# Where SyncE issues the stores of a weight conversion that runs inside attention

## The chip, the core and the metric

One core of a Trainium2 chip. Lower is better: the metric is the device time of one execution in microseconds (us), the median of the runs of a kernel. Names used below: TensorE (PE in the profile, its weight loads PEld), VectorE (DVE), ScalarE (ACT), GpSimd (POOL), SyncE (SP; it computes nothing and issues transfers, and rows of its queue are marked SPq).

## What is computed

Attention with its heads mixed before and after the softmax, and behind it a two-layer network on the result, all in float32:

```python
scores = scale * np.matmul(q, k.transpose(0, 1, 3, 2))
scores = np.einsum('bhij,hg->bgij', scores, w_pre)
attn = np.exp(scores - np.max(scores, axis=-1, keepdims=True))
attn = attn / (np.sum(attn, axis=-1, keepdims=True) + 1e-09)
attn = np.einsum('bhij,hg->bgij', attn, w_post)
x = np.matmul(attn, v)          # (8, 12, 448, 64), then reordered to (3584, 768)
h = x @ w_in                    # (768, 2048)
out = (h - np.tanh(h)) @ w_out  # (2048, 768)
```

The weights `w_in` and `w_out` come as float64. The chip computes on float32, so each weight is first turned into two float32 parts whose sum it is.

## The kernel before

**Two stages.** Attention runs first, on queries in blocks of 120 or 88 rows, and the network behind it, seven products in place of eight for a pair of token blocks. The conversion of the weights has nothing to do with attention. It is threaded into attention's work so that VectorE, ScalarE and GpSimd do it beside what they do for attention.

**Places.** Attention is a loop of 180 places (`for p in range(NPL + 3)`, L1256). In place `p` TensorE mixes the heads of two groups of score rows (`premix`, L918, into PSUM), VectorE takes their maximum (L927), ScalarE the exponential (L929), VectorE and GpSimd make the weights of the second mixing out of the sums (`norm`: VectorE L938 and L939, then GpSimd `wr` L940), and TensorE does the second mixing for place `p - 1` (`mix`, L957). Score blocks (L874) and products with v (L999) fill the rest of TensorE's time. A call `in_order` (L134) fixes that each engine, SyncE too, works in the order in which the program was written.

**Transfers.** The score rows that `premix(p)` needs are gathered by SyncE into one of six buffers `t` (L907, two transfers a place), in place `p - 2`; a buffer becomes free when the `premix` three places before has read it. All other transfers go through lists: `queue` (q, k, v, and the results `xs`) and `slow` (everything of the conversion). `dma` appends an entry with the number of the present place, and `issue(6)`, called right behind the two gathers of a place, sends up to six entries that are older than the place's new number, first those of `queue`, then those of `slow` (L769 to L773, sent in `send`, L766). `conv.place()` stands ahead of the place's count in L1262, so what it appends is sent in the same place. `now()` (L1032) empties the lists; it is used before and behind the places.

**The conversion.** There are 48 quads (a quad is four blocks of 128 by 128 weights), 24 of `w_in` and then 24 of `w_out`. `Convert.place()` starts a quad about every 3.25 places, at least three places apart, and carries each one on by one step a place:

- place k: VectorE L81, L82 on the loaded tile `cr`
- place k+1: GpSimd L84, ScalarE L85
- place k+2: VectorE L90, L91, L94; L90 is the first write to the quad's tile `co`
- place k+3: GpSimd L96, L97
- place k+4: ScalarE L100, and GpSimd's sums (L116 to L119, or L128 to L130), the first write to the tile `ct`
- place k+5: GpSimd L103 and L105, then the entry of the store of `co` (L106)
- place k+6: GpSimd L108, then the entry of the store of `ct` (L109)

```python
    nc.gpsimd.tensor_sub(ol, m, raw(oh))                                    # L103
    ...
    dma(dst, raw(o).rearrange("p x t n -> p x (t n)"))                      # L106
    yield
    nc.gpsimd.tensor_sub(t[:, :, 1].bitcast(F32R), t[:, :, 1], t[:, :, 0])  # L108
    dma(sums_dst, t.rearrange("p s t n -> p s (t n)"))                      # L109
```

`co` and `ct` have two buffers each (`bufs=2`), `cr` has three. The first write to a buffer waits until the store that last read it has landed: L90 of a quad waits for the store of `co` of the quad two before it. Both stores and both loads of a quad (512 KB each store, 256 KB each load) are entries of the one list `slow`.

Of the kernel before, what the change touches and what calls it, by code (L numbers as in the profile page):

```python
# [21 lines left out]
def raw(ap):  # L22

    return ap.bitcast(F32)
# [10 lines left out]
class Convert:  # L35


    def __init__(self, nc, pool, dma, items, places):
        self.nc, self.pool, self.dma = nc, pool, dma
        self.todo, self.loads, self.active = list(items), [], []  # L40
        self.rate, self.due = len(self.todo) / places, 1.0

# [7 lines left out]
    def place(self):  # L50
        for x in list(self.active):
            next(x[0], None)
            x[1] += 1
            if x[1] == 7:
                self.active.remove(x)
        self.due = min(self.due + self.rate, 1.3)
        if self.due >= 1.0 and len(self.active) < 2 and not [x for x in self.active if x[1] < 4] and self.loads and self.loads[0][1]():
            r, _, to = self.loads.pop(0)
            self.active.append([narrow_quad(self.nc, self.pool, self.dma, r, *to), 1])
            next(self.active[-1][0])  # L60
            self.due -= 1.0
        if self.todo and len(self.loads) < 2 and len(self.loads) + len([x for x in self.active if x[1] < 5]) < 3:
            self.load()
# [5 lines left out]
            between()  # L69


def narrow_quad(nc, pool, dma, r, dst, sums, sums_dst):

    p = r.shape[0]
    hi, lo = r[:, :, :, 1], r[:, :, :, 0]
    u, w = hi, lo


    lim = 122879.9921875
    m = pool.tile([p, 4, 128], F32, name="cm", tag="cm", bufs=2)  # L80
    nc.vector.tensor_scalar(m, hi.bitcast(F32), lim, -lim, op0=ALU.min, op1=ALU.max)  # L81
    nc.vector.tensor_scalar(w, lo, 8, None, op0=ALU.logical_shift_right)  # L82
    yield
    nc.gpsimd.tensor_scalar(m, m, 2.0**-112, None, op0=ALU.mult)  # L84
    nc.scalar.mul(w.bitcast(F32), w, 2.0**-44)  # L85
    yield
    o = pool.tile([p, 4, 2, 128], F32R, name="co", tag="co", bufs=2)
    oh, ol = o[:, :, 0], o[:, :, 1]
    s = ol.bitcast(I32)
    nc.vector.tensor_scalar(s, hi, -(2**31), None, op0=ALU.bitwise_and)  # L90
    nc.vector.scalar_tensor_tensor(  # L91
        out=u, in0=m.bitcast(I32), scalar=3, in1=s, op0=ALU.logical_shift_left, op1=ALU.bitwise_or
    )
    nc.vector.tensor_scalar(s, u, -(2**23), None, op0=ALU.bitwise_and)  # L94
    yield
    nc.gpsimd.tensor_tensor(out=m, in0=w.bitcast(F32), in1=s.bitcast(F32), op=ALU.mult)  # L96
    nc.gpsimd.tensor_tensor(out=m, in0=m, in1=u.bitcast(F32), op=ALU.add)  # L97
    yield
    t = pool.tile([p, 4, 2, 128], F32, name="ct", tag="ct", bufs=2)
    nc.scalar.copy(oh, m)  # L100
    done = sums(nc, m, t[:, :, 1])
    yield
    nc.gpsimd.tensor_sub(ol, m, raw(oh))  # L103
    done()
    nc.gpsimd.tensor_copy(t[:, :, 0].bitcast(F32R), t[:, :, 1])  # L105
    dma(dst, raw(o).rearrange("p x t n -> p x (t n)"))  # L106
    yield
    nc.gpsimd.tensor_sub(t[:, :, 1].bitcast(F32R), t[:, :, 1], t[:, :, 0])  # L108
    dma(sums_dst, t.rearrange("p s t n -> p s (t n)"))  # L109


def sums_in(nc, m, t):
# [38 lines left out]
def kernel_body(  # L151
# [11 lines left out]
    nc = tc.nc  # L163
# [38 lines left out]
    quads = []  # L202
# [97 lines left out]
    class Gate:  # L300

        def __init__(self, h, own_mask=True):
            self.h, self.own_mask = h, own_mask
# [66 lines left out]
    class Results:  # L370
# [145 lines left out]
        def store(self, b, t, h, c):  # L516
            to = out[b * TB + t * TT : b * TB + (t + 1) * TT, h * N2 : (h + 1) * N2]
            eng = nc.gpsimd if self.n_gr < len(self.grs) else nc.sync
            eng.dma_start(to, c.rearrange("p c n -> p (c n)"))
# [216 lines left out]
    with ExitStack() as st:  # L736
# [4 lines left out]
        cv = early.enter_context(tc.tile_pool(name="cv", bufs=1, side="left"))  # L741
# [12 lines left out]
        kks, vts, krs, qrs, qbs, sts, ats = {}, {}, {}, {}, {}, {}, {}  # L754


        queue, slow, sent = [], [], {}

        def dma(dst, src, to=None):
            entry = [place[0], dst, src, None]  # L760
            (queue if to is None else to).append(entry)
            return lambda places=0: entry[3] is not None and entry[3] + places <= place[0]

        def send(x, engine):
            entry = x.pop(0)
            engine.dma_start(*entry[1:3])  # L766
            entry[3] = place[0]

        def issue(most):  # L769
            for x in (queue, slow):  # L770
                while x and most and x[0][0] < place[0]:
                    send(x, nc.sync)
                    most -= 1  # L773

        place = [0]

        def load_k(b, hq, t=None):
            if t is None:
                t = ld.tile([CP, NC, 4, D], F32, name="kr", tag="kr", bufs=2)

            sent[b, hq, "k"] = dma(t, k[b, 4 * hq : 4 * hq + 4].rearrange("h (p c) d -> p c h d", c=NC))
            krs[b, hq] = t

        def load_v(b, hq):
            t = kp.tile([CP, 4, NC, D], F32, name="vr", tag="vr", bufs=3)
            sent[b, hq, "v"] = dma(
                t.rearrange("p h c d -> p h (c d)"),
                v[b, 4 * hq : 4 * hq + 4].rearrange("h (p c) d -> p h (c d)", c=NC),
            )
            vts[b, hq] = t  # L790

        def load_q(i, t=None):
            b, m = blocks[i]
            if t is None:
                t = ld.tile([MT, H, D], F32, name="qr", tag="qr", bufs=1)
            sent[i, "q"] = dma(t[: sizes[m]], q[b, :, starts[m] : starts[m] + sizes[m], :].rearrange("h p d -> p h d"))
            qrs[i] = t
# [234 lines left out]
        def now(*engines):  # L1032
            place[0] += 1
            engines = engines or (nc.sync,)
            for x in (queue, slow):
                while x:
                    send(x, engines[len(x) % len(engines)])


        load_q(0)  # L1040
        now()
        for hq in range(3):
            load_k(0, hq, kp.tile([CP, NC, 4, D], F32, name="tmp_k", tag="x", bufs=1) if hq == 2 else None)
        now()
        load_q(1, kp.tile([MT, H, D], F32, name="tmp_q", tag="at", bufs=2))
        now()
        for hq in range(3):
            load_v(0, hq)
# [32 lines left out]
        for w in range(2):  # L1081
            for at in AT[w]:
                x = repeat[:, w, at : at + HP].rearrange("p (i h) -> p i h", i=GH)
# [7 lines left out]
        for w in range(2):  # L1091
            for a in range(2):
                if w == 0:
                    x = both[:, w, a].rearrange("p (i g) -> p i g", i=GH)
                    of, step = ps_w[:, w, :].unsqueeze(1).to_broadcast([P, GH, H]), [[H, GH], [0, H]]
                else:
                    x = both[:, w, a].rearrange("p (g i) -> p g i", i=GH)
# [41 lines left out]
        place[0] += 1  # L1139
        scores_of(1, 0)  # L1140
        NPL = NG // 2
        conv = Convert(nc, cv, partial(dma, to=slow), quads, NPL - 24)

# [19 lines left out]
        at_s, p, kind = {}, 0, None  # L1165
        window = {i: (lo, hi) for lo, hi, k, i, _ in sorted(halved, reverse=True) if k == "s"}
        while halved:
            ready = sorted((x for x in halved if x[0] <= p), key=lambda x: (x[1], x[3:]))
            if ready:
                x = ready[0]  # L1170
# [3 lines left out]
                if x[2] == kind and other and x[1] > p + 1:  # L1174
                    x = other[0]
                halved.remove(x)
                _, _, kind, i, n = x
# [23 lines left out]
        for i, (b, m) in enumerate(blocks):  # L1201
            p0 = first[i] // 2
            if i + 2 < len(blocks):
                p = at_s[i + 2, 0] - 1
# [7 lines left out]
        for b in range(1, B):  # L1212
            p, o, done = first[blocks.index((b - 1, 1))] // 2 - 4, 0, []
            for hq in range(3):
                if hq == 2:

                    p = max(p, done[0] + 1)
                at_place(p, load_k, b, hq)
                o = max(p + 4, o + 1)
                p += 1  # L1220
                if hq > KB - 4:

                    o = max(o, end_s[blocks.index((b - 1, 3)), hq - 1 - (KB - 4)] + 1)
# [32 lines left out]
        for p in range(NPL + 3):  # L1256
# [6 lines left out]
            for t in (2 * p + 4, 2 * p + 5):  # L1263
                if t < NG:
                    gather(t)
            issue(6)
            if p == NPL + 1:
                for f in start.pop(p):
# [56 lines left out]
    for s in range(NS):  # L1325
# [24 lines left out]
        n = HELD[s] + AHEAD[s]  # L1350
# [44 lines left out]
```

## Time and profile before

| | |
|---|---|
| median of 3 runs | 1708.94 us (1706.41 to 1719.01) |
| the profiled execution | 1703.0 us, its span 1701.3 us |
| granted TensorE clock, mean | 0.994 |
| TensorE busy | 1660.1 us, 98% of the span |
| VectorE, ScalarE, GpSimd busy | 1231.3, 1091.1, 585.5 us |
| places, first to last `premix` | 25.2 to 838.8 us |
| the conversion, first L81 to last store issued | 51.5 to 781.5 us |

The page gives the busy time of each engine, the waits give for each engine and line how long it stood still and what ended that, in total, with the number of times and the longest. The timeline lists instructions by start and duration in us; a row of SPq is the time in which SyncE issues a transfer, not that of the transfer. The chain of work that ended last also has pieces that begin with DMA: a transfer from its issue to its landing.

### The profile page before, as it was taken

How to read it: one execution, taken by the hardware profiler on the slowest of the kernel's cores; microseconds unless marked ns; L12 is line 12 of the kernel's file. 1: busy time of each engine (PE TensorE's matmuls, PEld its weight loads, DVE VectorE, ACT ScalarE, POOL GpSimd, SP SyncE). 2: the span in 40 equal slices, each digit the busy share in tenths (PEclk: the TensorE clock that was granted, in tenths of full speed). 3: DMA queues.
4: the chain of work that ended last, by engine and by line, in shares of the span. 5: the costliest groups of instructions: out<-in, count | busy, mean ns of one | idle time of the engine just before them, and what ended most of it. 6: DMA issues, size and time to landing. Idle time of an engine off the chain costs nothing.

```text
span 1701.3 us, 41215 instructions
## 1 busy us (share of the span) xinstructions
PE 1660.1 (98%) x16068; PEld 1379.8 (81%) x16068; DVE 1231.3 (72%) x2119; ACT 1091.1 (64%) x1920; POOL 585.5 (34%) x798
## 2 busy tenths in 40 slices
PE   8999999999999899999999999999999999999999
PEld 6777777777777677677788888888888888989999
DVE  5777777878777777675497899868778867778432
ACT  5777777777777677676586777556667456666331
POOL 1466667666666666662100111101001101011100
PEclk9999999999999999999999999999999999999999
DMA  8879889898987979856589899989999989988993
GB/s 183 218 228 257 255 246 276 247 270 259 256 253 231 269 234 257 254 182 208 190 269 340 273 331 318 346 295 335 318 334 362 368 272 327 326 311 327 404 413 132
DMA packets 322290, 475.09 MB, mean 279 GB/s; under 512 B 105264, under 2 KB 255280, under 8 KB 322096
## 3 DMA queue, kind: packets, MB, share of 16 engines
q1 hardware_dynamic: 305660, 414.34, 75.5%
q0 software_dynamic: 16128, 57.68, 8.7%
q8 instruction: 128, 2.10, 0.5%
q14 instruction: 66, 0.54, 0.1%
q10 hardware_dynamic: 308, 0.43, 0.1%
HBM read 274.73 MB, written 120.59 MB: 232 GB/s over the span
## 4 chain that ended last, share of the span: by engine, by line
PE 72%; DMA 7%; DVE 7%; ACT 4%; issue 4%; POOL 4%; SPq 1%; POOLq 0%; ACTq 0%; DVEq 0%
PE ps_o L957 11%; PE ps_h L291 8%; PE ps_h L292 7%; PE ps_h L294 7%; PE ps_m L999 6%; PE ps_p L918 6%; PE y L534 6%; PE y L532 6%; PE y L533 6%; PE ps_q L874 4%; DMA t<-s 2%; DMA gl<-gs 2%; ACT e L929 1%; DVE mx L927 1%; PE y L504 1%
## 5 line engine op out<-in xcount | busy, mean ns | idle before, releaser
L957 PEld LDWEIGHTS ps_o<-wr,e 60*112 60x112 f32 (+1 forms) x5760 | 303.3, 175 | 46.1 <-POOL wr L940 31.9
L957 PE MATMUL ps_o<-wr,e 60*112 60x60 f32 (+1 forms) x5760 | 314.5, 259 | 16.1 <-POOL wr L940 14.6
L929 ACT ACTIVATE e<-ps_p,mx 128x448 f32<-128x448 f32 x360 | 224.8, 631 | 117.2 <-DVE mx L927 82.8
L927 DVE TENSOR_REDUCE mx<-ps_p 128x1 f32<-128x448 f32 x360 | 206.5, 615 | 109.1 <-PE ps_p L918 108.5
L967 ACT COPY at<-ps_o 112x960 f32<-112x960 f32 x156 | 154.3, 989 | 103.4 <-PE ps_o L957 102.9
L918 PE MATMUL ps_p<-t,wpre 60*64 60x448 f32 (+1 forms) x1440 | 182.4, 570 | 6.7 <-DMA t<-s 6.6
L999 PEld LDWEIGHTS ps_m<-at,vr 112*64 112x64 f32 x3072 | 147.6, 137 | 23.0 <-issue 7.7
L999 PE MATMUL ps_m<-at,vr 112*64 112x120 f32 (+1 forms) x3072 | 161.4, 262 | 1.1 <-DMA vr<-in_v_dram 0.9
L532 PE MATMUL y<-w,gh 128*128 128x384 f32 x448 | 151.2, 338 | 2.1 <-DMA w<-wo 1.6
L940 POOL TENSOR_TENSOR wr<-wpost,zs 128x120 f32<-128x120 f32 x180 | 70.0, 389 | 237.6 <-DVE zs L939 199.0
L533 PE MATMUL y<-w,gh 128*128 128x384 f32 x448 | 150.5, 336 | 0.0
L534 PE MATMUL y<-w,gl 128*128 128x384 f32 x424 | 143.4, 338 | 3.0 <-DVE gl L450 3.0
L874 PEld LDWEIGHTS ps_q<-kk,qh 64*120 64x120 f32 (+1 forms) x768 | 59.1, 174 | 82.0 <-issue 45.1
L874 PE MATMUL ps_q<-kk,qh 64*120 64x448 f32 (+1 forms) x768 | 121.8, 394 | 0.9 <-ACT kk L825 0.4
L879 DVE COPY s<-ps_q 120x448 f32<-120x448 f32 (+1 forms) x192 | 112.2, 614 | 9.8 <-PE ps_q L874 8.0
L669 POOL DMA_DIRECT2D gs<-gb x24 | 17.2, 717 | 291.6 <-DVE gb L668 291.6
L307 ACT ACTIVATE u<-h 128x1024 f32<-128x1024 f32 x56 | 59.5, 1063 | 74.4 <-DVE h L716 70.5
L879 ACT COPY s<-ps_q 120x448 f32<-120x448 f32 (+1 forms) x192 | 94.9, 538 | 7.1 <-PE ps_q L874 6.7
L647 POOL DMA_DIRECT2D gs<-ga x24 | 17.2, 716 | 230.0 <-DVE ga L330 222.9
L532 PEld LDWEIGHTS y<-w,gh 128*128 128x128 f32 x448 | 84.2, 188 | 7.2 <-issue 3.5
L533 PEld LDWEIGHTS y<-w,gh 128*128 128x128 f32 x448 | 84.1, 188 | 3.4
L534 PEld LDWEIGHTS y<-w,gl 128*128 128x128 f32 x424 | 79.6, 188 | 4.6 <-DVE gl L450 4.6
(372 smaller groups left out, 3971.3 us busy)
## 6 DMA issues: line engine op xcount, KB each, us to landing
t<-s SPq DMA_DIRECT2D x342, 210.0 KB
wa<-ss SPq DMA_DIRECT2D x96, 384.0 KB
w<-wo SPq DMA_DIRECT2D x43, 768.0 KB
gl<-gs SPq DMA_DIRECT2D x62, 512.0 KB
wa<-wi SPq DMA_DIRECT2D x72, 384.0 KB
w<-ts SPq DMA_DIRECT2D x35, 768.0 KB
gs<-gs POOLq DMA_DIRECT2D x24, 768.0 KB, 9.2
cr<-in_moe_w_in_dram SPq DMA_DIRECT2D x48, 256.0 KB
```

The lines of the kernel that those rows point to most:

```text
L291: nc.tensor.matmul(ph, w[:, c, 0], xh, start=start and c == 0, stop=False, skip_group_check=True)
L532: nc.tensor.matmul(y, gh[:, tok], wh, start=first, stop=False, skip_group_check=True)
L533: nc.tensor.matmul(y, gh[:, tok], wl, start=False, stop=False, skip_group_check=True)
L534: nc.tensor.matmul(y, gl[:, tok], wh, start=False, stop=last, skip_group_check=True)
L874: nc.tensor.matmul(ps[:n, :S], qx[a, hp, :], kx[a, hp % 2], start=(x == 0), stop=(x == 2))
L879: eng(sts[i][:n, 2 * hp + j, :], ps[:n, :S])
L918: nc.tensor.matmul(pss[r][halves[j], :], wpre[k, :], ts[j][k, :], start=True, stop=True)
L927: nc.vector.tensor_reduce(out=mx, in_=ps, axis=AX.X, op=ALU.max, negate=True)
L929: nc.scalar.activation(e, ps, AF.Exp, bias=mx, scale=1.0, accum_out=zs[:, 0, r : r + 1])
L957: nc.tensor.matmul(ps[:CP, j, c * GP : (c + 1) * GP].rearrange("p (h i) -> p h i", i=GI)[:, :, r * GH : (r + 1) * GH], e[k, c * CP : (c + ...
L967: nc.scalar.copy(ats[i0][:, :, :, at : at + 2 * GI].rearrange("p c h (j i) -> p j (c h) i", j=2), ps[:CP, :, : NC * GP].rearrange("p j (x ...
L999: nc.tensor.matmul(pv[j * D : (j + 1) * D, r, :n], vt[:, j, c, :], ats[i][:, c, 2 * hp + j, :n], start=(c == 0), stop=(c == NC - 1),)
```

## The change

The stores of the conversion get a list of their own, `out_q`, and an entry in it carries the number of the next place. `issue` and `now` serve it between `queue` and `slow`. A store is therefore sent one place later than the step that made its data, and the loads of the conversion, alone now in `slow`, are sent behind a store that falls due in the same place. No operation of a computing engine is added, removed or moved.

```diff
-    def __init__(self, nc, pool, dma, items, places):
-        self.nc, self.pool, self.dma = nc, pool, dma
+    def __init__(self, nc, pool, dma, store, items, places):
+        self.nc, self.pool, self.dma, self.store = nc, pool, dma, store
...
-            self.active.append([narrow_quad(self.nc, self.pool, self.dma, r, *to), 1])
+            self.active.append([narrow_quad(self.nc, self.pool, self.store, r, *to), 1])
...
-def narrow_quad(nc, pool, dma, r, dst, sums, sums_dst):
+def narrow_quad(nc, pool, store, r, dst, sums, sums_dst):
...
-    dma(dst, raw(o).rearrange("p x t n -> p x (t n)"))
+    store(dst, raw(o).rearrange("p x t n -> p x (t n)"))
     yield
     nc.gpsimd.tensor_sub(t[:, :, 1].bitcast(F32R), t[:, :, 1], t[:, :, 0])
-    dma(sums_dst, t.rearrange("p s t n -> p s (t n)"))
+    store(sums_dst, t.rearrange("p s t n -> p s (t n)"))
...
-        queue, slow, sent = [], [], {}
-
-        def dma(dst, src, to=None):
-            entry = [place[0], dst, src, None]
+        queue, slow, out_q, sent = [], [], [], {}
+
+        def dma(dst, src, to=None, behind=0):
+            entry = [place[0] + behind, dst, src, None]
...
         def issue(most):
-            for x in (queue, slow):
+            for x in (queue, out_q, slow):
...
         def now(*engines):
...
-            for x in (queue, slow):
+            for x in (queue, out_q, slow):
...
-        conv = Convert(nc, cv, partial(dma, to=slow), quads, NPL - 24)
+        conv = Convert(nc, cv, partial(dma, to=slow), partial(dma, to=out_q, behind=1), quads, NPL - 24)
```

The orders of TensorE, VectorE, ScalarE and GpSimd are the same in both programs; only SyncE's differs. It has two places below, in each of which two gathers (`t<-s`) open a place. The first is the place at about 151 us of the trace, where v and the next k are also loaded. `wi` is where the parts of `w_in` go, `ss` their sums. Before:

```order
L907 DMA t<-s 120x1x448 x2
L766 DMA qr<-in_q_dram 88x12x64
L766 DMA vr<-in_v_dram 112x4x256
L766 DMA wi_66<-co 512x1x256
L907 DMA t<-s 120x1x448 x2
L766 DMA vr<-in_v_dram 112x4x256
L766 DMA ss_78<-ct 512x1x256
L907 DMA t<-s 120x1x448 x2
L766 DMA kr<-in_k_dram 112x16x64
L766 DMA cr<-in_moe_w_in_dram 128x2x256 x2
```

With the change, from the same two gathers on:

```order
L907 DMA t<-s 120x1x448 x2
L766 DMA qr<-in_q_dram 88x12x64
L766 DMA vr<-in_v_dram 112x4x256
L907 DMA t<-s 120x1x448 x2
L766 DMA vr<-in_v_dram 112x4x256
L766 DMA wi_66<-co 512x1x256
L907 DMA t<-s 120x1x448 x2
L766 DMA kr<-in_k_dram 112x16x64
L766 DMA ss_78<-ct 512x1x256
L766 DMA cr<-in_moe_w_in_dram 128x2x256 x2
```

The store of `co` stands behind one more pair of gathers and a load of v. The store of `ct` now falls into the place of the next quad's two loads, and ahead of them. The second is the stretch that follows, before:

```order
L766 DMA cr<-in_moe_w_in_dram 128x2x256 x2
L907 DMA t<-s 120x1x448 x2
L766 DMA wi_67<-co 512x1x256
L907 DMA t<-s 120x1x448 x2
L766 DMA ss_79<-ct 512x1x256
L907 DMA t<-s 120x1x448 x2
L766 DMA cr<-in_moe_w_in_dram 128x2x256 x2
```

and with the change:

```order
L766 DMA cr<-in_moe_w_in_dram 128x2x256 x2
L907 DMA t<-s 120x1x448 x4
L766 DMA wi_67<-co 512x1x256
L907 DMA t<-s 120x1x448 x2
L766 DMA ss_79<-ct 512x1x256
L766 DMA cr<-in_moe_w_in_dram 128x2x256 x2
```

Where quads follow each other at three places, each place had one kind of the conversion's transfers (loads, `co`, `ct`); now one place has none, one has `co`, and one has `ct` and both loads.

## The prediction, as it was put on record

> **What bounds the kernel now.** The page comes first: TensorE is busy for 98% of the span. The second row below is that of the stretch 41 to 776 us in the view of windows (length, then the busy time of TensorE, its weight loads, VectorE, ScalarE and GpSimd), which holds nearly all of the conversion: 715.6 of 735 us.
>
> ```profile
> PE 1660.1 (98%) x16068; PEld 1379.8 (81%) x16068; DVE 1231.3 (72%) x2119; ACT 1091.1 (64%) x1920; POOL 585.5 (34%) x798
> ```
>
> ```profile
> 41.00:776.00 735.00, 715.59 (x10448) 549.17 (x10450) 547.42 (x1379) 528.20 (x1209) 483.75 (x615) 0.99 0.83 247
> ```
>
> So 19.4 us of that stretch are TensorE's idle time, and a change that leaves its work alone can win no more there. What ended that idle time stands in the waits of TensorE from 40 to 840 us (total, times, longest):
>
> ```profile
> PE ps_o L957 <- POOL wr L940: 13.4, 16, 1.7
> PE ps_p L918 <- DMA t<-s: 5.0, 7, 1.0
> ```
>
> The first row is the second mixing waiting for its weights, which come from VectorE over GpSimd. The second is the first mixing waiting for a gather that landed late. SyncE can shorten only the second: 5.0 us. Next, the waits in SyncE's own queue in the same stretch:
>
> ```profile
> SPq L907 <- PE ps_q L874: 130.4, 69, 5.0
> SPq L907 <- PE ps_p L918: 26.2, 28, 2.2
> ...
> SPq L766 <- POOL co L103: 14.4, 9, 4.4
> SPq L766 <- POOL ct L108: 13.1, 11, 4.7
> ```
>
> SyncE does stand before its transfers of L766 until GpSimd is done, 27.5 us in the two rows of the stores' own last steps, and it is in order, so the gathers of the next place stand behind it. But a gather mostly waits longer for TensorE to free its buffer (the first two rows).
>
> **What the change removes: SyncE's wait for GpSimd.** The timeline around 534 us shows one such wait and what it costs, first SyncE's rows, then one of GpSimd and one of TensorE:
>
> ```profile
> 530.33 2.03 SPq L907 DMA_DIRECT2D t<-s  x2
> 534.33 0.58 SPq L766 DMA_DIRECT2D ts<-ct  x1
> 535.89 1.59 SPq L907 DMA_DIRECT2D t<-s  x2
> ```
>
> ```profile
> 533.03 1.28 POOL L108 TENSOR_TENSOR ct<-ct 128x512 fp32r<-128x512 f32 x1
> ```
>
> ```profile
> 534.84 0.98 PE L918 MATMUL ps_p<-t,wpre 60*64 60x448 f32 x8
> ```
>
> SyncE is free at 532.36 and issues the store at 534.33, when L108 has ended (533.03 + 1.28 = 534.31): 1.97 us of waiting. It is free again at 534.91. The next gather goes out at 535.89 only, since the `premix` that frees its buffer ends at 534.84 + 0.98 = 535.82. Without the store's wait it would go out at the same time. This follows from the way a place is built: the gathers of a place need the `premix` of the place before, and GpSimd's step, recorded ahead of that `premix`, is over by then. So I take 0 us for the removed wait; the bounds are 0 and the 5.0 us by which TensorE waits for gathers at all. The issuing itself is only moved, 96 stores of some 0.6 us.
>
> **What the change moves: the stores land one place later.** A place lasts (838.8 - 25.2) / 179 = 4.55 us, from the first and last `premix` of 180:
>
> ```profile
> L918 PEld LDWEIGHTS ps_p<-t,wpre x1440: 128/132/229, 25.2 to 838.8; 60*64 60x64 f32 x172, 48*64 48x64 f32 x8
> ```
>
> ```profile
> L90 DVE TENSOR_SCALAR co<-cr x48: 407/418/1023, 59.2 to 761.5; 128x512 int32<-128x512 int32 x48
> ```
>
> L90 of a quad overwrites the `co` buffer of the quad two before, and must wait until that buffer's store has landed. Read off the timeline, 46 such pairs run from 8.3 to 18.9 us between the store's issue and L90, 13.5 us in the middle, and ten of them have 8.3 to 11.0 us. No wait of VectorE for a store of `co` is among its waits before, so all 46 fit. Take away a place and the ten are left with 3.8 to 6.5 us. (`ct` is first written two steps later than `co` and stored one later: it has a place more in hand, and I take 0 for it.) Two of the tightest pairs, with what hangs on L90 in each:
>
> ```profile
> 150.74 1.91 SPq L766 DMA_DIRECT2D wi<-co  x1
> ...
> 155.24 0.57 SPq L766 DMA_DIRECT2D ss<-ct  x1
> ...
> 159.46 0.41 DVE L90 TENSOR_SCALAR co<-cr 128x512 int32<-128x512 int32 x1
> ...
> 161.60 0.39 POOL L940 TENSOR_TENSOR wr<-wpost,zs 128x120 f32<-128x120 f32 x1 [2.66 <-DVE zs L939]
> ...
> 163.59 1.69 PE L957 MATMUL ps_o<-wr,e 60*112 60x60 f32 x32
> ```
>
> ```profile
> 567.12 0.44 SPq L766 DMA_DIRECT2D wo<-co  x1
> ...
> 570.14 6.12 SPq L766 DMA_DIRECT2D ts<-ct  x1
> ...
> 575.44 0.42 DVE L90 TENSOR_SCALAR co<-cr 128x512 int32<-128x512 int32 x1
> ...
> 578.07 0.39 POOL L940 TENSOR_TENSOR wr<-wpost,zs 128x120 f32<-128x120 f32 x1
> ...
> 581.31 0.87 PEld L957 LDWEIGHTS ps_o<-wr,e 60*112 60x112 f32 x16 [0.16 <-issue]
> ```
>
> In both, the store of `co` goes with the change to about where the store of `ct` stands now: 155.24 and 570.14. VectorE is then 4.2 and 5.3 us from L90. Behind L90 in VectorE's order stand L938 and L939, for these GpSimd's `wr`, for that TensorE's mixing. The first pair has 163.59 - 161.99 = 1.6 us to spare between `wr` and the mixing, the second 581.31 - 578.46 = 2.85. What L90 waits beyond that, TensorE waits too.
>
> How long does a store take to land? The trace tells it only where a transfer is on the chain of work that ended last (start, us from issue to landing):
>
> ```profile
> 156.75 9.32 DMA t<-s
> 194.27 3.24 DMA wi<-co
> 565.65 6.48 DMA t<-s
> 581.96 3.99 DMA wo<-co
> ```
>
> Stores in a quiet stretch: 3.24 and 3.99 us. Gathers in just the two crowded stretches above: 9.32 and 6.48 us. They give the bounds. With the place's 4.55 us added and compared with the 46 distances:
>
> - 3.24 us for all: no pair is short, 0 us.
> - 6.48 us: the ten tight pairs are short by 10.6 us in all; less 1.6 us to spare each time, 2.8 us reach TensorE.
> - 9.32 us: 26 pairs are short by 53.5 us, and 23.4 us reach TensorE.
>
> The tight pairs lie in crowded stretches (v, k and q are loaded there, and one issue took 6.12 us), so the nearest row is the crowded gather of the same stretch, 6.48 us, and I take 2.8 us. [...]
>
> **What it bunches.** The order of SyncE shows one place in three with a store of `ct` and both loads of the next quad, where each place had one kind. The gathers behind them land later, those of the empty place earlier. The bounds are the 5.0 us of TensorE's present waits for gathers, lost once more or won. Bunching leans to the loss; I take a fifth, 1.0 us.
>
> **Sum.** 0 + 2.8 + 1.0 = 3.8 us. On the profiled execution, 1703.0 us (span 1701.3), that is 1706.8 us. The median of the runs shown, 1708.94, lies 5.9 us above this execution, so I predict 1708.94 + 3.8 = 1712.7, put as 1713 us. A measurement of this kernel can tell about 1% (17 us) from no change; I forecast none that it can tell.
>
> **The rivals.**
>
> - *A lost transfer wait:* the conversion's wait was what made gathers late, and TensorE's 5.0 us go away: 1704 us. For it: the 27.5 us of SyncE's waits for GpSimd. Against it: around 534 us the gather's buffer sets the time.
> - *Nothing:* late stores land in 3.2 us as in the quiet rows, and L90 never waits: 1709 us. [...] Against it: the issue of 6.12 us and the 9.32 us landing.
> - *The reuse of `co` becomes the wait, everywhere:* stores take 9.32 us, VectorE stops at 26 of 46 quads, 23.4 us reach TensorE, with the bunching's 5.0 us 1737 us: slower. The point from which it decides is a landing of about 8.7 us in all pairs: by the same count 16.8 us reach TensorE there, 1%. For it: the first crowded row. Against it: two thirds of the pairs have more than 12 us and lie in quiet stretches, where the rows say 3.2 to 4.0.
> - *The change does not do what it says*, since `issue` sends six entries at most and a store could be pushed on: excluded by SyncE's order, where each store is exactly one place on.
>
> **How the numbers follow.** The forecast (a few L90 waits, 1709 to 1722 us) 0.60; nothing 0.18; gathers won 0.13; the reuse decides 0.08; a gain of over 1% 0.01, as it would need nearly all of the 19.4 us of idle time. The first three lie within 1%, 0.91, and I move a little to each side for what two medians of few runs differ by: faster 0.02, same 0.90, slower 0.08. The range goes down to the rival that wins gathers with a little of the runs' spread (1703) and up to a landing of 8 us in all pairs (10.0 us) with a part of the bunching (1723).
>
> **What would show it.** Right: in the changed kernel's waits a row of VectorE `co` L90 waiting for a DMA of `co`, about five to ten times with some 10 us in all, mostly near 160, 270, 380, 575 and 690 us; SyncE's rows of L766 waiting for GpSimd L103 and L108 nearly gone; TensorE's wait of L957 for `wr` some 2 to 5 us up, its wait for gathers between 3 and 8 us; and the last `premix` 2 to 8 us later than 838.8 us. The step on the removed wait is wrong if the gather row falls below 2 us. The step on `co` is wrong if VectorE never waits for a store there. The forecast as a whole is wrong if the time leaves 1703 to 1723 us.

## The result, and the profile after

| | before | after |
|---|---|---|
| median (10 runs each, taken together) | 1707.12 us | 1720.91 us |
| lowest to highest | 1702.51 to 1719.01 | 1709.83 to 1728.38 |
| the profiled execution | 1703.0 us | 1727.89 us |
| its span, its granted clock | 1701.3 us, 0.994 | 1726.2 us, 0.983 |

The ratio of the two kernels is 1.0063, with an interval from 1.0034 to 1.0092: the change costs 10.8 us (5.8 to 15.7). The medians alone differ by 13.8 us, inside that interval. The profiled execution of after is one of its longer runs.

**What one run's two numbers tell.** Each run lists its span and its mean granted clock. The table below splits the span into span x clock, about the time that the run would have taken at the full clock, since TensorE sets the time for nearly all of it (busy for 98% of the span of before, 97% of that of after), and span x (1 - clock), the time that the lower clock took. In after the first part lies between 1695.8 and 1699.6 us in all ten runs, so most of their spread, 18.5 us, is the clock. Means, with the standard deviation of one run:

| | runs | at the full clock | lost to the clock |
|---|---|---|---|
| before (beside the experiments) | 73 | 1692.5 us (1.5) | 14.5 us (3.4) |
| after | 10 | 1697.3 us (1.4) | 22.2 us (6.4) |
| difference | | +4.8 us | +7.7 us |

Three more runs of before, 1 to 7% longer at a lower clock, are left out of the 73. The first difference has an error of some 0.5 us, the second of some 2 us (the deviations over the square root of the number of runs). So the change costs in two ways, and for the second, which looks like the larger one, the prediction had no term.

**Where the profile of after shows it.** The last `premix` of attention, from the view of TensorE's line L918:

```profile
L918 PEld LDWEIGHTS ps_p<-t,wpre x1440: 129/132/228, 25.8 to 863.2; 60*64 60x64 f32 x172, 48*64 48x64 f32 x8
```

It was at 838.8 us before: 24.4 us, all but half a microsecond of the difference of the two executions (1726.2 - 1701.3 = 24.9), arise in attention. TensorE's waits there, from 40 us to the last `premix`:

```profile
PE ps_o L957 <- POOL wr L940: 16.4, 19, 2.3
PE ps_p L918 <- DMA t<-s: 5.3, 4, 2.0
PE ps_m L999 <- DMA vr<-in_v_dram: 3.3, 3, 2.2
```

The mixing's wait for `wr` went from 13.4 to 16.4 us, the gathers' from 5.0 to 5.3, and the product with v waits 3.3 us for its load, 0.9 before:

```profile
PE ps_m L999 <- DMA vr<-in_v_dram: 0.9, 1, 0.9
```

Together that is 25.0 against 19.3 us, 5.7 us more of standing still, about what the full-clock time says. Each row is that of one execution, though. In the kernels below in which SyncE's order is that of before (e6, e8, e9 and e11), TensorE waits 2.1 to 4.6 us for v, so the 3.3 us alone do not show an effect of the change. VectorE's waits in the same stretch of after:

```profile
DVE x L1017 <- DMA xs<-x: 5.3, 3, 3.2
DVE co L90 <- DMA wi<-co: 4.5, 4, 2.9
DVE co L90 <- DMA wo<-co: 2.8, 2, 2.5
```

The last two rows did not exist before: L90 stands six times, 7.3 us in all, until a store of `co` has landed. (The first row, 1.0 us before and 1.3 to 6.4 us in the four kernels just named, is a result of attention waiting for its buffer.) One of the six can be followed to TensorE, first in SyncE's timeline, then in that of the others:

```profile
159.68 0.51 SPq L766 DMA_DIRECT2D vr<-in_v_dram  x1
160.30 0.56 SPq L766 DMA_DIRECT2D wi<-co  x1
...
163.07 0.83 SPq L766 DMA_DIRECT2D kr<-in_k_dram  x1
164.00 5.22 SPq L766 DMA_DIRECT2D ss<-ct  x1
```

```profile
168.30 0.43 DVE L90 TENSOR_SCALAR co<-cr 128x512 int32<-128x512 int32 x1 [2.92 <-DMA wi<-co]
...
170.15 0.17 DVE L939 RECIPROCAL zs<-zs 128x2 f32<-128x2 f32 x1
170.46 0.39 POOL L940 TENSOR_TENSOR wr<-wpost,zs 128x120 f32<-128x120 f32 x1 [8.13 <-DVE zs L939]
...
170.90 0.80 PE L957 MATMUL ps_o<-wr,e 60*112 60x60 f32 x12 [2.33 <-POOL wr L940]
```

The store goes out at 160.30 between loads of v and k and releases L90 at 168.30, 8.0 us later. L90 waited 2.92 us for it, and two steps further TensorE has waited 2.33 us for `wr`. What follows is in the view of windows (length, busy time of TensorE, its weight loads, VectorE, ScalarE and GpSimd, then the granted clock, the DMA share and GB/s):

```profile
169.70:173.10 3.40, 2.20 (x40) 1.86 (x40) 2.98 (x11) 2.17 (x7) 2.64 (x3) 1.00 1.00 293
173.20:176.50 3.30, 3.30 (x30) 2.47 (x24) 1.31 (x3) 2.62 (x7) 3.14 (x7) 0.50 0.74 255
```

Behind the gap the granted clock is 0.50 for a stretch. So the wait cost its 2.33 us, and about half of 3.4 us once more, if the stretch is put down to it. In the profiled execution of after, such stretches up to the end of attention make up 16 times 3.41 us, in that of before 5 times: 11 x 1.7 = 18.8 us of the 24.4. That is more than the 7.7 us of the means: this execution of before lost less to the clock than most (10.4 us in its whole span), and this one of after more (29.0 us).

### The profile page after: what moved, and what is told of

Its sections match the earlier page's. It is cut to its first block, busy times and chain, and to the rows that moved or that the text cites. A ratio compares the mean times of both kernels' runs of the same rounds, so it can differ in the third digit from the quotient of the medians.

```text
span 1726.2 us, 41222 instructions
## 1 busy us (share of the span) xinstructions
PE 1678.0 (97%) x16068; PEld 1392.2 (81%) x16068; DVE 1233.7 (71%) x2119; ACT 1091.9 (63%) x1920; POOL 585.0 (34%) x798
## 4 chain that ended last, share of the span: by engine, by line
PE 74%; DVE 7%; DMA 7%; ACT 4%; issue 4%; POOL 3%; SPq 1%; POOLq 0%; ACTq 0%; DVEq 0%
PE ps_o L957 11%; PE ps_h L291 7%; PE ps_h L292 7%; PE ps_h L294 7%; PE ps_m L999 7%; PE ps_p L918 6%; PE y L532 6%; PE y L534 6%; PE y L533 6%; PE ps_q L874 4%; DMA wi<-co 2%; DMA t<-s 2%; ACT e L929 1%; DVE mx L927 1%; DMA w<-wo 1%
## 5 line engine op out<-in xcount | busy, mean ns | idle before, releaser
L957 PEld LDWEIGHTS ps_o<-wr,e 60*112 60x112 f32 (+1 forms) x5760 | 308.2, 177 | 50.2 <-POOL wr L940 35.7
L957 PE MATMUL ps_o<-wr,e 60*112 60x60 f32 (+1 forms) x5760 | 319.5, 261 | 18.9 <-POOL wr L940 17.6
L918 PE MATMUL ps_p<-t,wpre 60*64 60x448 f32 (+1 forms) x1440 | 185.7, 581 | 7.2 <-DMA t<-s 6.9
L999 PEld LDWEIGHTS ps_m<-at,vr 112*64 112x64 f32 x3072 | 152.0, 140 | 27.5 <-issue 8.8
L999 PE MATMUL ps_m<-at,vr 112*64 112x120 f32 (+1 forms) x3072 | 166.4, 266 | 3.4 <-DMA vr<-in_v_dram 3.3
L879 DVE COPY s<-ps_q 120x448 f32<-120x448 f32 (+1 forms) x192 | 112.6, 615 | 10.8 <-PE ps_q L874 10.1
```

The source lines that it names most:

```text
L879: eng(sts[i][:n, 2 * hp + j, :], ps[:n, :S])
L918: nc.tensor.matmul(pss[r][halves[j], :], wpre[k, :], ts[j][k, :], start=True, stop=True)
L957: nc.tensor.matmul(ps[:CP, j, c * GP : (c + 1) * GP].rearrange("p (h i) -> p h i", i=GI)[:, :, r * GH : (r + 1) * GH], e[k, c * CP : (c + ...
L999: nc.tensor.matmul(pv[j * D : (j + 1) * D, r, :n], vt[:, j, c, :], ats[i][:, c, 2 * hp + j, :n], start=(c == 0), stop=(c == NC - 1),)
```

## The experiments

The experiments of each group ran beside runs of the kernel before on the same chip; a ratio is to these. In the three groups the mean full-clock time of before is 1692.2, 1692.8 and 1692.5 us. The table sums the experiments up, as differences from the means of before above; an error of some 0.4 to 1.4 us belongs to the full-clock column and of 1 to 4 us to the other.

| kernel | runs | median | ratio (95%) | at full clock | lost to the clock |
|---|---|---|---|---|---|
| after | 10 | 1720.91 | 1.0063 (1.0034 to 1.0092) | +4.8 | +7.7 |
| e1_co3 | 12 | 1713.86 | 1.0044 (1.0021 to 1.0068) | +2.8 | +3.5 |
| e3_co_late | 6 | 1723.13 | 1.0103 (1.0065 to 1.0141) | +7.7 | +8.5 |
| e4_ct_late | 12 | 1710.13 | 1.0018 (0.9998 to 1.0038) | +0.1 | +2.2 |
| e5_two_late | 5 | 1753.01 | 1.026 (1.0238 to 1.0283) | +15.6 | +27.9 |
| e6_before_co3 | 12 | 1712.55 | 1.0007 (0.9987 to 1.0027) | +0.5 | +2.5 |
| e7_co_late_co3 | 7 | 1725.31 | 1.0086 (1.0054 to 1.0117) | +6.9 | +10.2 |
| e8_stall | 12 | 1711.14 | 1.0011 (0.9991 to 1.0031) | +2.0 | +0.8 |
| e9_norm_first | 6 | 1738.97 | 1.0155 (1.0126 to 1.0184) | +22.4 | +6.4 |
| e10_spread | 12 | 1711.03 | 1.0015 (0.9992 to 1.0038) | +0.9 | +1.8 |
| e11_before_fill | 12 | 1703.25 | 0.9961 (0.994 to 0.9982) | +2.5 | -7.7 |
| e12_after_fill | 12 | 1713.80 | 1.0015 (0.999 to 1.0041) | +6.9 | -2.5 |

The list `out_q` by itself, without the later number, leaves SyncE's order as it was before; it was not run. What is tested is the later place.

### e1_co3: the change with a third buffer of co

```diff
-    o = pool.tile([p, 4, 2, 128], F32R, name="co", tag="co", bufs=2)
+    o = pool.tile([p, 4, 2, 128], F32R, name="co", tag="co", bufs=3)
```

> The changed kernel with three co buffers in place of two, so that L90 waits for the store of the quad three before. Reuse theory (the late store of co makes VectorE wait at L90, TensorE stands still behind it, and the clock is granted at half after it): no wait of L90 for a DMA of co, and 0 to 4 us over the kernel before, where the change has 10.8. Bunching theory (the store of ct together with both loads makes gathers and loads of v land late): unchanged by the buffer, 8 to 14 us over before.

Measured: 1713.86 us. There is no row of L90 waiting for a store any more, and TensorE's waits are:

```profile
PE ps_o L957 <- POOL wr L940: 12.9, 15, 1.6
PE ps_p L918 <- DMA t<-s: 4.7, 5, 1.3
PE ps_m L999 <- DMA vr<-in_v_dram: 2.4, 3, 1.3
```

The wait for `wr` is back at what it was before (13.4). Against after, 2.0 us of full-clock time are gone (error 0.7) and 4.2 us of lost clock (error 2.6). So the reuse of `co` is real, and its stops have about the size that the prediction gave them; but 2.8 us of full-clock time stay, so it is not all. By the ratio e1 lies 7.5 us over before, between the ranges of the two theories.

### e3_co_late and e4_ct_late: one of the two stores late

```diff
-    store(sums_dst, t.rearrange("p s t n -> p s (t n)"))
+    store(sums_dst, t.rearrange("p s t n -> p s (t n)"), behind=0)
```

is e3: only `co` is late, and falls into the place of `ct`. In e4 the same `behind=0` stands at the store of `co` (L106): only `ct` is late, and falls into the place of the loads.

> Only the store of co goes a place later, that of ct stays in time; both then fall into one place, and the loads have a place of their own. Reuse theory: as the change, L90 waits 5 to 10 times, 5 to 10 us in all, 6 to 14 us over before. Bunching of ct with the loads: not there, 0 to 4 us over before.

> Only the store of ct goes a place later, into the place of the next quad's loads; that of co stays in time. Reuse theory: no wait of L90 for a DMA of co, 0 to 3 us over before. Bunching theory: 6 to 14 us over before, with TensorE's waits for gathers and for v at 8 us or more (6 us before).

Measured: e3 1723.13 us, e4 1710.13 us. With `co` alone late the kernel loses more full-clock time than with the whole change (+7.7 against +4.8 us), and by its ratio, 17.6 us over before, it lies above the ranges of both theories. L90 waits twice there, 5.8 us in all, and not 5 to 10 times. What both stores of a quad, 1 MB, in one place cost is the subject of e7. With `ct` alone late, 33 places hold `ct` and both loads, exactly as many as in after, and the mean full-clock time is that of before (+0.1 us, error 0.8). So on the mean those places by themselves are not what costs. Yet e4's profile shows the waits that the bunching theory had named, for v and gathers 11.0 us (8 or more were expected), TensorE's and then VectorE's from 40 to 850 us:

```profile
PE ps_m L999 <- DMA vr<-in_v_dram: 5.6, 5, 2.3
PE ps_p L918 <- DMA t<-s: 5.4, 6, 1.4
```

```profile
DVE x L1017 <- DMA xs<-x: 5.6, 3, 3.3
```

The profiled execution has 1696.0 us of full-clock time, 3.5 more than the mean of before; the twelve runs of e4 go from 1689.0 to 1698.0 us. So in that execution the waits cost time, and the other runs of e4 need not have had them. A profile of one execution does not say what a kernel pays on the mean.

### e5_two_late: both stores two places late

```diff
-partial(dma, to=out_q, behind=1)
+partial(dma, to=out_q, behind=2)
```

> Both stores two places later in place of one. The 46 distances from the store of co to L90 lose another 4.5 us and are 2 to 10 us, against a landing of 5.7 us at the median. Reuse theory: L90 waits at half of the quads or more, 50 us or more of VectorE's time in all, and 25 to 60 us over before. Bunching theory: co in place of ct now falls in with the loads, the same amount, 8 to 14 us over before.

Measured: 44 us more. VectorE's and TensorE's waits from 40 to 890 us:

```profile
DVE co L90 <- DMA wi<-co: 16.7, 9, 4.8
DVE co L90 <- DMA wo<-co: 15.3, 5, 5.3
```

```profile
PE ps_o L957 <- POOL wr L940: 37.8, 22, 6.4
```

L90 waits 14 times, 32.0 us in all, fewer and less than expected (half of the quads, 50 us), and TensorE's wait for `wr` goes from 13.4 to 37.8 us. The time is in the range of the reuse theory. This is the rival in which the reuse decides, brought on by a second place. Of the 44 us, 27.9 are lost clock, where after, with 16.4 us of waits for `wr`, loses 7.7.

### e6_before_co3: the third buffer without the change

This is the kernel before with the one line of e1.

> The kernel before with three co buffers, SyncE's order as before: a control for the third buffer itself. If the 7 us that are left in the changed kernel with three buffers come from where the stores stand, this is 0 to 2 us from before, and the time at full clock (span times granted clock) within 1.5 us of the 1692 us of before. If the third buffer costs something by itself, 4 us or more over before.

Measured: ratio 1.0007, the interval on both sides of 1. The buffer by itself makes no difference that these runs can tell, so what e1 wins over after is the wait it takes away.

### e7_co_late_co3: co late, with the wait taken away

This is e3 with the one line of e1.

> Only the store of co late, with three co buffers: the kernel that alone cost 17.6 us, without the reuse. Reuse theory: no wait of L90 for co, time at full clock 3 us or less over before (8 us with two buffers), 2 to 7 us over before in all. Crowding theory (co and ct, 1 MB, in one place): time at full clock still 5 us or more over before, 10 us or more in all.

Measured: 1725.31 us, not better than e3. Its waits for transfers, TensorE's from 40 to 850 us, then VectorE's:

```profile
PE ps_m L999 <- DMA vr<-in_v_dram: 7.6, 6, 2.0
PE ps_p L918 <- DMA t<-s: 7.1, 6, 2.5
```

```profile
DVE x L1017 <- DMA xs<-x: 6.2, 3, 3.0
```

No L90 waits, and the wait for `wr` is 14.0 us, near that of before. TensorE's two waits are the largest of their kind in all the kernels here. In e6, which has the same three buffers and SyncE's order of before, the three rows are 2.1, 4.3 and 1.7 us: TensorE waits 8.3 us longer for v and gathers in e7, near the 6.9 us of the means. So in e7, where both stores of a quad stand in one place, TensorE stands longer for the transfers of attention (14.7 against 6.4 us), and SyncE's order sets a price on its own, without any wait for a buffer of the conversion. What the third buffer wins against e3 (0.8 us of full-clock time, error 1.5) can't be told.

### e8_stall: the stops alone

The kernel before with 13 more operations of VectorE ahead of L90 in five of the six quads where after stops. Their results are not used.

```diff
+STALL = {7: 5, 14: 1, 15: 2, 22: 1, 35: 4}
...
+    for _ in range(STALL.get(n, 0)):
+        x = pool.tile([p, 4, 128], F32, name="cx", tag="cx", bufs=1)
+        nc.vector.tensor_scalar(x, hi.bitcast(F32), lim, -lim, op0=ALU.min, op1=ALU.max)
```

> The kernel before, with 13 extra VectorE operations of about 0.6 us on a tile of their own ahead of L90 in five quads (5 in the eighth, 4 in the 36th, 2 in the 16th, one each in the 15th and 23rd): some 8 us of VectorE's time where the changed kernel had its waits of L90, and no transfer moved. Theory (a stop of VectorE ahead of zs stops TensorE, and a gap on TensorE costs granted clock as well): time at full clock 3 to 6 us over before, granted clock lower by 0.001 to 0.004, in all 4 to 12 us over before. If it is the transfers alone: 0 to 2 us.

Measured: the operations take 6.6 us in all, by the groups of instructions,

```profile
L96 DVE TENSOR_SCALAR cx<-cr 128x512 f32<-128x512 f32 x13 | 6.6, 505 | 0.3
```

close to the 7.3 us by which L90 waits in after. The full-clock time rises by 2.0 us (error 0.5), what e1 took off: about a third of these stops of VectorE reached TensorE. That is less than the 3 to 6 us expected, and by the ratio the whole, 1.9 us, misses the 4 to 12 us of the theory. The lost clock hardly moves (+0.8 us, error 0.9), where e1 against after gave 4.2 us. That difference is within the errors, but e8 does not show that such stops cost clock.

### e9_norm_first: the norm ahead of the conversion

The kernel before, with `norm(p - 1)` moved ahead of `conv.place()`, so that L938, L939 and `wr` no longer stand behind L90.

> The kernel before with norm (zs on VectorE, wr on GpSimd) recorded ahead of the conversion's step of a place, so that L90, L91 and L94 no longer stand ahead of zs. If TensorE's gaps before L957 (13.4 us in 16 waits) come from that order and drag the clock: TensorE's waits for wr 6 us or less, granted clock up by 0.002 or more, 6 to 20 us faster than before. If VectorE or the exponential only get late elsewhere: within 4 us of before, or slower.

Measured: 1738.97 us, a miss. The wait for `wr` does fall, but other waits rise, TensorE's from 40 to 880 us and one of VectorE's:

```profile
PE ps_p L918 <- ACT e L929: 15.1, 17, 1.5
PE ps_o L957 <- POOL wr L940: 4.8, 10, 1.2
```

```profile
DVE zs L938 <- ACT e L929: 20.0, 50, 0.9
```

L938 reads the sums of the exponential, and moved forward it stands for ScalarE (20.0 us, 9.5 before) with the conversion behind it. TensorE's waits in attention account for some 9 us of the 22.4; the rest stands in the profile as busy time of TensorE (L918 201.7 us, 182.4 before), and why stays open. What the run shows is that the stop at L90 ahead of `norm` is cheaper than the other order.

### e10_spread: late, but spread and with spare buffers

After, with the store of `ct` two places late in place of one, and three buffers each of `co` and `ct`. Again most places have one kind of the conversion's transfers: 37 places have `ct` alone (15 in after), 11 have it with the loads (33 in after).

```diff
-    store(sums_dst, t.rearrange("p s t n -> p s (t n)"))
+    store(sums_dst, t.rearrange("p s t n -> p s (t n)"), behind=2)
```

> The changed kernel with co one place late and ct two places late, three buffers of each: late as in the change, but where quads follow at three places each place again has one kind of the conversion's transfers, and no buffer is short. Crowding theory: time at full clock within 2 us of before's 1692.5, 0 to 4 us over before in all (the changed kernel with three co buffers: 6 to 7). If lateness itself costs: 6 us or more over before.

Measured: ratio 1.0015, no difference that these runs can tell. TensorE's waits for transfers and the results' row:

```profile
PE ps_p L918 <- DMA t<-s: 5.2, 5, 1.8
PE ps_m L999 <- DMA vr<-in_v_dram: 1.2, 2, 0.9
```

```profile
DVE x L1017 <- DMA xs<-x: 1.8, 1, 1.8
```

The waits for v and `xs` are near those of before. So lateness by itself costs nothing measurable (0.38% at most by the interval), and gains nothing either: what costs here is the buffer that it holds (2.0 us of full-clock time, after less e1) and the transfers that it brings together (1.9 us, e1 less e10). The third buffer of `ct` was not run by itself. What it can take away against e1 is one wait of GpSimd for a store of `ct`, 2.1 us; behind it GpSimd stands 1.2 us for VectorE ahead of the next `wr`, so in that execution the wait did not reach TensorE.

### e11_before_fill and e12_after_fill: the gaps filled

Both kernels with 33 small products of TensorE ahead of the second mixing in eight places, in which TensorE had stood for about 1 to 1.7 us. Their results are overwritten.

```diff
+        FILL = {17: 5, 28: 3, 40: 5, 118: 4, 124: 5, 145: 3, 150: 5, 179: 3}
...
+            for _ in range(FILL.get(p, 0)):
+                nc.tensor.matmul(ps[:, 0, :P], ident, ident, start=True, stop=True)
```

> The kernel before with 33 matmuls of 128 by 128 that compute nothing (0.22 us each, into the bank that the mixing then overwrites) ahead of the mixing of eight places where TensorE stands for 1.0 to 1.7 us for wr in every trace: they fill most of these gaps and move no other work. Clock theory (a gap on TensorE brings stretches at half clock): mean granted clock up by 0.002 to 0.006, 3 to 10 us faster than before. If the clock does not hang on the gaps: clock as before, 0 to 2 us slower.

> The changed kernel with the same 33 matmuls. Clock theory: 3 to 10 us faster than the changed kernel, so 1 to 8 us over before, granted clock up by 0.002 to 0.006 over the changed kernel's 0.987. If the clock does not hang on the gaps: 10 to 13 us over before.

Measured: e11 1703.25 us, 0.39% faster than before (0.18 to 0.6%), the only kernel here that is. The wait for `wr` (now at L961) in its profile:

```profile
PE ps_o L961 <- POOL wr L940: 5.5, 15, 0.6
```

TensorE has more to do, and the full-clock time rises by 2.5 us; the lost clock falls from 14.5 to 6.8 us. In the kernel after the same products take it from 22.2 to 12.0 us, and cost 2.1 us. This is the test of the second term: with gaps filled and no transfer moved, the clock comes back. e12 stays slower than e11 by some 10 us (4.4 of full-clock time, 5.2 of clock). The change's own stops are still in it: in its profile L90 waits 6.8 us for stores of `co`, and the wait for `wr` is 9.1 us.

## Why the prediction was right, and where not

The time lies in the range, and within 1% of before, as the likeliest case had it. That it does so is partly luck. The sum was 3.8 us, a third of the 10.8 us measured; the range reached up to 1723 us for landings of 8 us and a part of the bunching, and what filled it was the clock, for which it had no term. The prediction also forecast no change that could be told from noise, and ten runs of each kernel do tell it. The steps:

**The removed wait is worth nothing: right.** The gathers' row stayed (5.0 to 5.3 us); no gain of SyncE reached TensorE. Nor was SyncE's wait quite removed. Its waits in after:

```profile
SPq L766 <- POOL co L103: 10.4, 5, 3.3
...
SPq L766 <- POOL ct L108: 2.2, 5, 0.6
```

The row of L108 nearly vanished (13.1 before), that of L103 did not (14.4 before). The prediction expected both to go. It stays open which transfers hold the 10.4 us: a row of L766 mixes all of SyncE's other transfers, and names the release that came last.

**The reuse of `co`: right in place and size.** Five to ten waits of some 10 us were expected; there are six, 7.3 us in all. They stand at 168, 276, 289, 395, 598 and 724 us, and five of the six quads are among the prediction's ten tight pairs, one at each place named; the whole execution is later by then. e1 and e8 each measure 2.0 us at TensorE for the 2.8 us of the sum. Two terms of it were off, and partly made up for each other. Where L90 waits, the store landed 6.1 to 8.9 us after its issue, mostly later than the 6.48 us taken. But VectorE came to L90 later too: in these five pairs 5.1 to 6.6 us after the issue, where the sum had left them 3.8 to 6.3. (For the second pair shown the prediction reads off 5.3 us and counts 3.8; it was 6.0.) The 0 us for `ct` held in the profile of after, which has no wait for a store of `ct`. In the quiet rows of before SyncE's stores took 3.24 and 3.99 us, less than any of these six.

**The bunching: right in sign, its cause not shown.** e1 less e10 gives 1.9 us of full-clock time (error 0.9) for where the transfers stand, for the 1.0 us of the sum, inside its bounds. The prediction saw the price in the gathers. In e7 it is in gathers and loads of v alike; in e1 no row shows it, since TensorE's waits there (12.9, 4.7 and 2.4 us) are near those of e6 (13.2, 4.3 and 2.1). And the prediction's picture of the cause, `ct` with both loads in one place, is not supported: e4 has the same places at +0.1 us. In e1, `co` is late as well and stands in the place just ahead of them. Why e1 pays and e4 does not stays open; the difference, 2.7 us, has an error of some 1.0 us.

**The sum: a term is missing.** 3.8 us were predicted, and 4.8 us measured as full-clock time. The whole came to 10.8 us because the clock granted behind TensorE's gaps was lower as well, and the sum counted a gap at its length alone. The number for it stood beside the profile of before: a granted clock of 0.994, that is 1701.3 x 0.006 = 10.2 us lost in that execution (14.5 us in the mean of all runs), more than the sum of the prediction's terms. For this reason too the last `premix` came 24 us later and not 2 to 8 in the profiled execution: 5.7 us of standing and 18.8 us of half clock, of which a part is only the difference between these two executions.

**The rivals.** A lost transfer wait and nothing fall with the rows above. The reuse deciding everywhere needs one place more, as e5 shows.

How the 12.5 us of the means divide: reuse 2.0 + 4.2 (after less e1), where the transfers stand 1.9 + 1.7 (e1 less e10), what is left in e10 0.9 + 1.8. The first numbers, full-clock time, are good to about 0.8 us, the second to 2.5 us only, so how the lost clock divides among the causes is not settled. That lost clock hangs on gaps of TensorE is shown by e11 and e12, which fill some, and by e5, which has more; that the 7.7 us of the change come from its own gaps fits this, but e8 did not show it for the stops alone.

## What to carry to other kernels

Where TensorE is the bound, price a new gap twice: its own length, and what the granted clock may lose behind it (in the one followed in after, 2.33 us and about half of the 3.4 us at 0.50); span x clock of each run separates the two, and was steadier here than the time (over the 73 runs of before a standard deviation of 1.5 us, against 3.8 us). Before a wait row of a few us is put down to a change, look at the same row in a kernel without it: here the wait for v ran from 0.9 to 4.6 us with SyncE's order untouched. A store sent later holds its buffer longer and lands beside other transfers: list the shortest distances to the buffer's next write, count them against the landing time of a crowded stretch (here 6.1 to 8.9 us) and not of a quiet one (3.24 and 3.99 us), and see what comes to share a place with it. Of the stops of a side engine TensorE felt only a part in e8, 2.0 of 6.6 us, and putting the waited-for work first may uncover another wait, as in e9 (L938 for ScalarE, 20.0 us against 9.5).

## What the runs showed of the clock

In the traces of before and after the granted clock is either 1.0 or 0.5, the latter in 7 stretches in before and 12 in after: of 3.41 us, in after also three of 6.83 and one of 10.24 us, and one of before cut off by the span's end. That one begins 3.3 us behind TensorE's last work, the others 1.3 to 4.6 us behind the start of a gap of TensorE of 1.0 to 2.3 us, but not every such gap has one.

The two traces say more on which gaps do. Within each, the starts of the stretches lie whole multiples of 3.4133 us apart, a third of the 10.24 us (in before they are at 25.10, 595.12, 694.11, 721.41, 844.29, 1588.40 and 1701.04 us). Cut each trace into windows on that grid, from its first stretch on. Behind a window at full clock in which TensorE was busy for less than 45% of the time, the half clock came in 4 of 4 cases, behind one with 45 to 75% in 13 of 31, and behind one with more in none of 930. So in these traces it counts where the grid cuts a gap. TensorE stands for 1.57 us ahead of L957 in before, and for 1.56 us at the same work in e1; the timeline, then the two windows around it, before and then e1:

```profile
210.31 1.78 PE L957 MATMUL ps_o<-wr,e 60*112 60x60 f32 x32 [1.57 <-POOL wr L940]
```

```profile
206.00:209.42 3.42, 2.74 (x36) 1.56 (x32) 2.82 (x8) 2.37 (x6) 0.32 (x1) 1.00 1.01 225
209.42:212.83 3.41, 2.52 (x40) 1.86 (x40) 3.38 (x8) 2.45 (x7) 2.96 (x3) 1.00 0.86 286
```

```profile
211.60:215.02 3.42, 1.86 (x28) 1.33 (x24) 3.25 (x10) 1.46 (x4) 1.30 (x2) 1.00 0.96 284
215.02:221.84 6.82, 6.82 (x54) 4.98 (x52) 4.95 (x13) 4.24 (x11) 6.61 (x9) 0.50 0.57 193
```

In before the gap, which begins at 208.74 us, falls into two windows, and the clock stays. In e1 it lies in one, TensorE is busy for 1.86 us of 3.42 there, and 6.82 us at half clock follow. But that is not the whole rule. Here another gap of 1.57 us ahead of L957, in before and then in after, which lies in one window in both, but for 0.06 us; the timeline, then the windows:

```profile
103.66 1.78 PE L957 MATMUL ps_o<-wr,e 60*112 60x60 f32 x32 [1.56 <-POOL wr L940]
```

```profile
100.19:103.60 3.41, 1.91 (x18) 0.73 (x16) 3.24 (x10) 1.54 (x3) 0.38 (x2) 1.00 1.04 281
103.60:107.02 3.42, 3.36 (x48) 2.53 (x50) 2.03 (x7) 2.74 (x6) 3.34 (x4) 1.00 0.81 278
```

```profile
104.26 1.02 PE L957 MATMUL ps_o<-wr,e 60*112 60x60 f32 x14 [1.57 <-POOL wr L940]
```

```profile
101.49:104.90 3.41, 1.84 (x27) 1.11 (x20) 3.24 (x10) 1.45 (x3) 1.08 (x2) 1.00 0.97 306
104.90:111.73 6.83, 6.83 (x54) 4.99 (x52) 2.99 (x8) 4.40 (x12) 5.12 (x8) 0.50 0.62 222
```

TensorE is busy for 1.91 and for 1.84 us of 3.41, and goes on at 1.00 in the one and at 0.50 in the other. The fullest window of the 13, in before at 690.70 us, has 71%. What decides between 45 and 75% stays open.
